# Attention with hash buckets and a small expert layer: whole-array shapes for two products, float16 experts, pairs of chunks on GpSimd

## The chip, the cores and the metric

The kernel runs on one core of a Trainium2 chip. The core has five engines with instruction streams of their own: TensorE (PE), VectorE (DVE), ScalarE (ACT), GpSimd (POOL) and SyncE (SP). They meet at semaphores. SBUF is the on-chip memory of 128 partitions, PSUM the memory that PE writes its products to, and queues carry DMA between device memory and SBUF. The metric is the device time of one execution in microseconds (us); lower is better.

## The reference

Inputs are q, k and v of shape (4, 8, 768, 64), that is 4 batches of 8 heads, 768 tokens and 64 dimensions, all float32, a projection of 64 by 6, a gate vector of 512, and the expert's weights w1 (512 by 1024) and w2 (1024 by 512).

```python
q_bucket = sum over 6 bits of (q @ proj > 0) * 2**bit       # k_bucket likewise
mask = q_bucket[..., :, None] == k_bucket[..., None, :]
scores = where(mask, q @ k.T / 8, -1e9)
scores = scores - max(scores, -1)
attn = exp(scores);  attn = attn / (sum(attn, -1) + 1e-9)
x = attn @ v                                # regrouped as (4, 768, 512)
for b in range(4):
    s = x[b] @ w_gate
    top = the 128 tokens of the highest s
    ye = relu(x[b, top] @ w1) @ w2
    out[b, top] = x[b, top] + sigmoid(s[top]) * ye     # other tokens: out = x
```

So there are 32 heads of attention with a mask, and after every eighth head one choice of 128 tokens and one small expert layer on them. Since the chosen tokens depend on a ranking of float32 sums, the kernel carries its products in pieces: a high part and a low part of float16 or bfloat16 stand for one float32.

## The kernel before, in words

**One head.** `load_x` brings q and k of a head, transposed, as one 128 by 768 tile X. `hash_half` and `signs` form the hash bits as +-8192 rows. `split_xh` (ACT) and `split_xl` (DVE, line 235) cut X into float16 parts XH and XL, and SP's DMAs place these in the operands A and B of a head (`place_a`, `place_b`). A score product over A thus holds the dimensions and the hash bits at once, so that equal buckets stand far above all others.

*The maxima.* For each of six chunks t of 128 queries `max_unit` makes two products mx of 384 columns; `max_relu` (ACT, line 348) takes the relu of the one, a difference of two halves of keys, and `max_red` (DVE, line 356, the rows mj) adds the other and leaves the maximum in a column of m. `max_turn` (line 365) turns m (128 by 6) with one product mt into six rows, `max_copy` (ACT) copies them into mr, and `max_row` sends them with a DMA of SP into row 96 of A. The difference of halves that A needs is `k_diff` (DVE, line 334, xd).

*The scores.* `st_unit` makes transposed scores st (keys in partitions) in nine units of 512 columns, each one product over A (line 385) and one over B (389); the row of maxima must be in A before the head's first. `st_exp` (ACT, lines 403 and 405) writes the exponentials into P, a float32 tile of two chunks of 128 keys, three units to a pair of chunks.

*The sum over v.* P is used as its upper 16 bits (read in place as bfloat16) and a rest R, P minus those 16 bits, as float16. `r_chunk` (line 418) makes R for each of the six chunks of keys, on DVE or on POOL; the table `POOL_R` names the chunks that POOL takes, by even and odd head. `av` multiplies both with v's parts (line 442, three products of 65 or 64 columns for each chunk and tile of queries) on top of a seed (line 428): a product of `zs` and `W` that starts all 396 columns of the accumulator with a multiple of the sum of v. `W` is 33 rows: row 0 holds the high part of that sum, row 32 the low part (`sum_hi`, `sum_lo`, line 319). `recip` (DVE, 452 to 454, the rows rc) and `norm` (ACT, line 467) divide.

**One batch.** `score` (DVE, line 484, rows jks) forms the gate's sums as heads finish. `choose` ranks 768 tokens by comparing every score with every other (lines 528 to 536, rows cm and eq), turns the rank into an index and gathers the 128 tokens with POOL's indirect DMA (606). `expert` does the layer: `turn_x` transposes the tokens (xp); `split_x` makes a float32r high part, a float32r rest and a bfloat16 copy; `up` (662) multiplies the tokens' parts with w1's parts, with the tokens as the stationary operand and 512 columns of w1 moving: 12 products for each half of the 1024 hidden values; `relu`, then `turn_h` transposes the hidden values with four products per half (674), `split_h` and `split_h2` cut them, `down` (700) multiplies with w2's parts, and `finish` (707) scales, adds and scatters. The experts of batches 0 and 1 are stepped between the heads of later batches, that of batch 2 runs at the end, and that of batch 3 must wait for the last head (`rank_last`, `apply_expert_last`).

**What sets the order.** Every step above is put on one list by a due time: head h starts its scores at 9h, and each kind of step has an offset in a table T. The steps are issued in the order of these due times, and every engine runs its own instructions in exactly that order. `mine` marks a DVE instruction, and `turn` makes the next POOL instruction wait for the one marked last. `LEAD` is how far the maxima run ahead of the scores, `AVLAG` how far `av` runs behind.

## Time and profile before

| | |
| - | - |
| time, median of 3 runs | 487.26 us (485.84 to 487.91) |
| the profiled execution | 488.31 us, of which the span of instructions is 486.5 |
| mean granted PE clock | 0.956 |
| busy: PE, DVE, ACT, POOL | 430.6, 396.5, 344.0, 171.7 us |
| largest groups on DVE | R 119.5, mj 106.2 us |
| largest groups on ACT | exponentials 113.2 and 58.0, relu 95.3 us |

A row of a group names the line, the engine, the operation, out<-in by the program's names, the shape, the count, the busy time and the mean of one in ns, and the idle time ahead of it with what ended it. A row of the timeline names the start in us, the duration, and in brackets the wait ahead of the instruction. Matmul rows include the pipeline's tail, so their starts, not their durations, tell how fast PE takes them. L418 is line 418 of the kernel.

### The profile page before, as it was taken

The page shows a single profiled execution, that of the slowest core. Times are in us where ns is not written, and L with a number is a line of the kernel's source. Part 1 is how long each engine was busy: PE and PEld are TensorE (multiplying, and loading weights), DVE is VectorE, ACT ScalarE, POOL GpSimd, SP SyncE. Part 2 cuts the span into 40 slices and gives each one's busy share as a digit, 9 for nine tenths or more (in the row PEclk, how much of TensorE's full clock was granted, in tenths as well). Part 3 has the DMA queues.
Part 4 walks back from the last instruction along what each step waited for, and adds up shares of the span by engine and source line. Part 5 has one row for each costly group of instructions (what it writes and reads, how often), then busy time and mean ns, then how long its engine had stood idle before and what let it go on. Part 6 is the DMA issues. An engine that isn't in the chain of part 4 may idle for free. (4 is left out here: it accounts for less than half of the span.)

```text
span 486.5 us, 14126 instructions
## 1 busy us (share of the span) xinstructions
PE 430.6 (89%) x5379; PEld 283.9 (58%) x5393; DVE 396.5 (81%) x991; ACT 344.0 (71%) x826; POOL 171.7 (35%) x137
## 2 busy tenths in 40 slices
PE   4789999978997898999998889899897899998795
PEld 3146666555654665676656566566565666666463
DVE  5669989999999997777799999999999977656611
ACT  2588898889885876787777579698775778763312
POOL 7025654445463352222413242324242333232300
PEclk9689999999999798999999899999998889999999
DMA  4774535545663233342464226445531133102010
GB/s 127 235 200 131 168 100 169 179 123 136 197 190 96 81 112 98 120 111 67 143 186 123 77 66 169 140 127 137 157 111 44 30 106 98 34 2 88 2 43 22
DMA packets 36167, 55.30 MB, mean 114 GB/s; under 512 B 6194, under 2 KB 27396, under 8 KB 36100
## 3 DMA queue, kind: packets, MB, share of 16 engines
q1 hardware_dynamic: 24676, 34.85, 26.2%
...
## 5 line engine op out<-in xcount | busy, mean ns | idle before, releaser
L418 POOL TENSOR_TENSOR R<-P 128x768 f16<-128x768 f32 x80 | 124.9, 1562 | 246.9 <-DVE xd L334 95.1
L403 ACT ACTIVATE P<-st 128x512 f32<-128x512 f32 x192 | 113.2, 608 | 37.1 <-PE st L389 35.2
L442 PEld LDWEIGHTS <-P 128*128 128x128 bf16 x2304 | 120.1, 99 | 30.2 <-issue 20.3
L442 PE MATMUL av<-V,P 128*128 128x65 f16 (+1 forms) x2304 | 128.0, 196 | 0.0
L442 PE MATMUL av<-V,R 128*128 128x65 f16 x1152 | 123.1, 194 | 3.9 <-POOL R L418 2.3
L418 DVE TENSOR_TENSOR R<-P 128x768 f16<-128x768 f32 x112 | 119.5, 1067 | 7.0 <-ACT P L405 6.8
L385 PE MATMUL st<-A 97*128 97x256 f16 (+1 forms) x384 | 123.4, 333 | 0.3
L389 PE MATMUL st<-B 128*128 128x256 f16 (+1 forms) x384 | 123.3, 333 | 0.0
L356 DVE CUSTOM_DVE_ANT_0 mj<-mx,me 128x384 bf16<-128x384 f32 x192 | 106.2, 553 | 20.8 <-PE mx L340 8.4
L348 ACT ACTIVATE me<-mx 128x384 f32<-128x384 f32 x192 | 95.3, 497 | 28.7 <-DVE m L356 14.0
L442 PEld LDWEIGHTS <-R 128*128 128x128 f16 x1152 | 108.5, 100 | 5.2 <-POOL R L418 2.7
L340 PE MATMUL mx<-K,A 96*128 96x384 f16 x192 | 60.7, 344 | 10.4 <-DVE oneb L159 4.7
L405 ACT ACTIVATE P<-st 128x512 f32<-128x512 f32 x96 | 58.0, 604 | 11.3 <-PE st L389 10.0
L340 PE MATMUL mx<-A 96*128 96x384 f16 x192 | 64.6, 338 | 1.4 <-ACT me L348 0.7
L340 PEld LDWEIGHTS <-A 96*128 96x128 f16 x384 | 36.3, 100 | 30.0 <-issue 12.2
L467 ACT ACTIVATE x<-av,rc 128x64 f32<-128x64 f32 x192 | 42.2, 311 | 12.1 <-DVE rc L454 11.9
L385 PEld LDWEIGHTS <-A 97*128 97x128 f16 x384 | 38.1, 99 | 21.2 <-issue 7.2
L389 PEld LDWEIGHTS <-B 128*128 128x128 f16 x384 | 38.3, 100 | 18.7 <-issue 1.9
L235 DVE SCALAR_TENSOR_TENSOR XL<-X,XH 128x768 f16<-128x768 f32 x32 | 39.7, 1242 | 2.3 <-DMA B<-XL 2.3
L230 ACT ACTIVATE XH<-X 128x768 f16<-128x768 f32 x32 | 27.1, 850 | 7.6 <-DMA X<-in_qk_dram 7.6
L203 PE MATMUL hp<-X,pjt 128*32 128x384 f32 x128 | 17.6, 524 | 1.9 <-DMA X<-in_qk_dram 1.8
L334 DVE TENSOR_TENSOR xd<-XH 64x384 f16<-64x384 f16 x32 | 12.7, 397 | 8.0 <-ACT XH L230 7.1
...
## 6 DMA issues: line engine op xcount, KB each, us to landing
...
```

Source lines behind the costliest of these rows:

```text
L230: nc.scalar.activation(xh, st["X", h], AF.Copy, scale=XS)
L235: mine(nc.vector.scalar_tensor_tensor(xl, st["X", h], XS, st["XH", h], op0=ALU.mult, op1=ALU.subtract))
L340: nc.tensor.matmul(pt[:, :384], a[0:96, 0, t * P : (t + 1) * P], a[0:96, 1, 384:768] if i else K[h % NA][0:96], start=True, stop=True,)
L348: nc.scalar.activation(me, st["mx", h, t, 0][:, :384], AF.Relu)
L356: nc.vector.tensor_tensor_reduce(out=jk, in0=st["mx", h, t, 1][:, :384], in1=st["me", h, t], op0=ALU.add, op1=ALU.max, scale=1.0 / MS, sca ...
L385: nc.tensor.matmul(pt[:, o : o + n], a[:, 1, c * P : (c + 1) * P], a[:, 0, q0 : q0 + n], start=True, stop=False,)
L389: nc.tensor.matmul(pt[:, o : o + n], bt[:, 1, c * P : (c + 1) * P], bt[:, 0, q0 : q0 + n], start=False, stop=True,)
L403: nc.scalar.activation(pp[:, r, 0:512], pt, AF.Exp, scale=ES)
L405: nc.scalar.activation(pp[:, :, 512:768], pt.rearrange("p (a b) -> p a b", a=2), AF.Exp, scale=ES)
L418: (turn if pool else mine)(eng.tensor_tensor(t, pp[:, r, :], hi_view(pp, r), op=ALU.subtract))
L442: nc.tensor.matmul(o[:, t, 0:n], l, vv[:, c, hh, v0 : v0 + n], start=False, stop=last and l is lo, skip_group_check=True,)
L467: nc.scalar.activation(x[:, t], o[:, t, 0:D], AF.Copy, scale=rc[:, t : t + 1])
```

## The change

**Shapes.** m is now one of two fixed 128 by 128 tiles M, zero but for six columns, so that the turning product has all 128 rows of output; the seed reads 65 rows of zs and W instead of 33, with the low part in row 64 (both are cleared at the start).

**Experts.** w1 and w2 are kept as a float16 part and a bfloat16 rest. The tokens are scaled by 16 and cut into two float16 parts. `up` now has the weights as the stationary operand and the tokens moving, 128 columns each: 48 products for each half, and the hidden values come out transposed, so `turn_h` is gone. `split_h` takes relu and high part on ACT and the rest on DVE. `down` has its 24 products of 512 columns as before.

**R.** POOL takes R in pairs of chunks with one instruction of 128 by 1536: chunks 2 and 3 of an even head, chunks 0, 1 and 4, 5 of an odd one. DVE takes the others, one chunk per instruction. R's tiles hold a pair, four of them.

**Order.** All of T is new, with LEAD, AVLAG and AVS, and the junk tile of mj has two buffers.

Three places in the order of the instructions show what moved. The first is DVE in head 22 and the start of head 23's work; R22_2 is the rest of head 22's chunk 2, mj24_1 the second chunk of maxima of head 24. Before:

```order
L418 TENSOR_TENSOR R22_0_6520<-P22_0_6442 128x768
L356 ISA mj23_5_6524,m23_6294<-mx23_5_1_6515,me23_5_6513 128x384
L334 TENSOR_TENSOR xd26_6530<-XH26_6522 64x384
L452 TENSOR_SCALAR rc21_6568<-av21_6344 128x6
L356 ISA mj24_0_6574,m24_6573<-mx24_0_1_6564,me24_0_6562 128x384
L235 SCALAR_TENSOR_TENSOR XL25_6580<-X25_5542,XH25_6240 128x768
L418 TENSOR_TENSOR R22_2_6604<-P22_1_6528 128x768
L356 ISA mj24_1_6606,m24_6573<-mx24_1_1_6599,me24_1_6597 128x384
L418 TENSOR_TENSOR R22_3_6644<-P22_1_6528 128x768
```

And now:

```order
L241 SCALAR_TENSOR_TENSOR XL25_6524<-X25_5251,XH25_6163 128x768
L462 TENSOR_SCALAR rc21_6528<-av21_6330 128x6
L362 ISA mj24_1_6534,M0_79<-mx24_1_1_6526,me24_1_6520 128x384
L362 ISA mj24_2_6539,M0_79<-mx24_2_1_6532,me24_2_6522 128x384
L362 ISA mj24_3_6575,M0_79<-mx24_3_1_6566,me24_3_6563 128x384
L426 TENSOR_TENSOR R22_2_6613<-P22_2_6536 128x768
L362 ISA mj24_4_6663,M0_79<-mx24_4_1_6632,me24_4_6628 128x384
L362 ISA mj24_5_6665,M0_79<-mx24_5_1_6634,me24_5_6630 128x384
L362 ISA mj25_0_6682,M1_80<-mx25_0_1_6678,me25_0_6676 128x384
L340 TENSOR_TENSOR xd27_6689<-XH27_6680 64x384
```

XL has moved ahead of three rc and three mj, and one R stands where three stood; the R of chunks 2 and 3 has left DVE. (Rows that read an accumulator, the other rc and score rows are left out; the last number of a name in the R rows of the change counts pairs.)

The second place is POOL at the same heads. Before:

```order
L418 TENSOR_TENSOR R22_1_6566<-P22_0_6442 128x768
L418 TENSOR_TENSOR R22_4_6697<-P22_2_6608 128x768
L418 TENSOR_TENSOR R23_1_6816<-P23_0_6708 128x768
L418 TENSOR_TENSOR R23_2_6854<-P23_1_6778 128x768
L418 TENSOR_TENSOR R23_4_6948<-P23_2_6858 128x768
```

And now:

```order
L429 TENSOR_TENSOR R22_1_6561<-P22_1_6435 128x1536
L429 TENSOR_TENSOR R23_0_6674<-P23_0_6606 128x1536
L429 TENSOR_TENSOR R23_2_6879<-P23_2_6784 128x1536
L429 TENSOR_TENSOR R24_1_7079<-P24_1_6947 128x1536
```

Five instructions of one chunk have become three of two. Each waits for the DVE instruction marked last ahead of it: the first for XL25 above, the second for the R ahead of mj24_4.

The third place is DVE at the end: sc3 are the last batch's scores, ye2 the result of batch 2's expert, cm3 the ranking of batch 3. Before:

```order
L842 TENSOR_TENSOR sc3_2_9190<-sc3_2_9190,sc3_1_9000 128x6
L653 TENSOR_SCALAR ss2_9181<-ss2_9181 128x1
L692 TENSOR_TENSOR htl2_9244<-ht2_0_9238,hth2_9243 128x512
L528 TENSOR_SCALAR cm3_0_9257,cnt3_9256<-sbc3_9205,sc3_2_9190 128x640
L882 TENSOR_SCALAR idx3_9331<-ip3_9318 128x1
L692 TENSOR_TENSOR htl2_9244<-ht2_1_9297,hth2_9243 128x512
L707 SCALAR_TENSOR_TENSOR ye2_9354<-yp2_9268,ss2_9181,xe2_8097 128x512
```

And now:

```order
L805 TENSOR_TENSOR sc3_2_9168<-sc3_2_9168,sc3_1_8948 128x6
L684 SCALAR_TENSOR_TENSOR htl2_9174<-mh2_0_9116,hth2_9173 128x512
L684 SCALAR_TENSOR_TENSOR htl2_9174<-mh2_1_9177,hth2_9173 128x512
L661 TENSOR_SCALAR ss2_9112<-ss2_9112 128x1
L701 SCALAR_TENSOR_TENSOR ye2_9279<-yp2_9230,ss2_9112,xe2_8139 128x512
L538 TENSOR_SCALAR cm3_0_9284,cnt3_9283<-sbc3_9244,sc3_2_9168 128x640
```

The whole expert of batch 2 now stands ahead of the ranking of batch 3, which it followed and was mixed with.

The diff, cut to its core:

```diff
+EX = 16.0
+KZ = 65
-LEAD = 14
-AVLAG = 3
+LEAD = 14.39
+AVLAG = 4.79
-AVS = ((0, 9, 1.1), (9, 18, 2.34), (18, 27, 5.75), (27, 36, 6.91))
+RB = 4
+AVS = ((0, 9, 1.9), (9, 18, 3.66), (18, 27, 5.56), (27, 36, 6.99))
 T = dict(
-    loadx=-34.22, hash=-5.11, hash2=4.23, sign=0.81, xh=-11.6, xl=-1.02, pa=-4.18, ps=2.13, loadv=-16.35,
+    loadx=-40.48, hash=-4.07, hash2=1.42, sign=1.08, xh=-10.75, xl=1, pa=-0.1, ps=2.23,
...
-POOL_R = ((1, 4), (1, 2, 4))
+POOL_R = ((1,), (0, 2))
...
-    zs = cp.tile([33, P], BF16, name="zs")
+    zs = cp.tile([KZ, P], BF16, name="zs")
+    M = [cp.tile([P, P], F16, name=f"M{i}") for i in range(2)]
...
-    w1h = cp.tile([P, 4, FF], F32R, name="w1h")
+    w1h = cp.tile([P, 4, FF], F16, name="w1h")
...
-        w = W[pr % 2][32:33, :, 0 : D + 1]
+        w = W[pr % 2][64:KZ, :, 0 : D + 1]
...
-            st["m", h] = sb.tile([P, NC], F16, tag="m", name=f"m{h}", bufs=2)
-        jk = sb.tile([P, 384], BF16, tag="jks", name=f"mj{h}_{t}", bufs=1)
+            st["m", h] = M[h % 2]
+        jk = sb.tile([P, 384], BF16, tag="jks", name=f"mj{h}_{t}", bufs=2)
...
-        nc.tensor.matmul(pt[:NC, :P], st["m", h], ident16, start=True, stop=True)
+        nc.tensor.matmul(pt[:, :P], st["m", h], ident16, start=True, stop=True)
...
     def r_chunk(h, c):
-        need(("e", h, 3 * (c // 2) + 2))
-        pp, r = st["P", h, c // 2], c % 2
-        t = sb.tile([P, S], F16, tag="R", name=f"R{h}_{c}", bufs=6)
-        pool = c in POOL_R[h % 2]
-        eng = nc.gpsimd if pool else nc.vector
-        (turn if pool else mine)(eng.tensor_tensor(t, pp[:, r, :], hi_view(pp, r), op=ALU.subtract))
-        st["R", h, c] = t
+        g, r = divmod(c, 2)
+        need(("e", h, 3 * g + 2))
+        pp = st["P", h, g]
+        if r == 0:
+            st["R", h, g] = sb.tile([P, 2, S], F16, tag="R", name=f"R{h}_{g}", bufs=RB)
+        t = st["R", h, g]
+        if g not in POOL_R[h % 2]:
+            mine(nc.vector.tensor_tensor(t[:, r], pp[:, r], hi_view(pp, r), op=ALU.subtract))
+        elif r == 0:
+            a = slice(0, 2)
+            turn(nc.gpsimd.tensor_tensor(t, pp, hi_view(pp, a), op=ALU.subtract))
...
-                st["O", h], zs, W[h // 2 % 2][:, hh].unsqueeze(1).broadcast_to([33, NC, OW]),
+                st["O", h], zs, W[h // 2 % 2][:, hh].unsqueeze(1).broadcast_to([KZ, NC, OW]),
...
         def split_x():
             xp = t["xp"]
-            xh, xl, xb = tile_("xth", 512, F32R), tile_("xtl", 512, F32R), tile_("xtb", 512, BF16)
-            nc.scalar.copy(xh, xp)
-            nc.vector.tensor_tensor(xl, xp, xh.bitcast(F32), op=ALU.subtract)
-            nc.scalar.copy(xb, xh.bitcast(F32))
-            t["x"] = ((xh, w1h), (xl, w1h), (xb, w1l))
-            t["hs"] = tile_("hs", FF, F32)
+            xh, xl = tile_("xth", 512, F16), tile_("xtl", 512, F16)
+            nc.scalar.activation(xh, xp, AF.Copy, scale=EX)
+            nc.vector.scalar_tensor_tensor(xl, xp, EX, xh, op0=ALU.mult, op1=ALU.subtract)
+            t["x"] = ((xh, w1h), (xl, w1h), (xh, w1l))
...
+        def up(hp, e, fs, order=(0, 1, 2)):
+            for i in order:
+                x, w = t["x"][i]
+                for f in fs:
+                    o = e * 512 + f * P
+                    for k in range(4):
+                        nc.tensor.matmul(
+                            hp[:, f * P : (f + 1) * P], w[:, k, o : o + P],
+                            x[:, k * P : (k + 1) * P],
+                            start=(f == 0 and k == 0 and i == order[0]),
+                            stop=(k == 3 and i == order[-1]), skip_group_check=True,
+                        )
+        def split_h(hp, e):
...
+            nc.scalar.activation(hh[:, f], hp, AF.Relu)
+            nc.vector.scalar_tensor_tensor(
+                hl[:, f], hp, 0.0, hh[:, f], op0=ALU.max, op1=ALU.subtract
+            )
...
     def apply_expert_last(b, tags, bank, bank2):
...
-        m.up(h0, 0, range(4), (0, 2, 1), True)
-        m.relu(h0, 0)
-        m.up(h1, 1, range(2), (0, 2, 1), True)
-        m.turn_h(bank(f"ht{b}_0"), 0)
...
+        m.up(h0, 0, range(4), (0, 2, 1))
+        m.split_h(h0, 0)
+        m.up(h1, 1, range(4), (0, 2, 1))
+        m.split_h(h1, 1)
```

More of the change, by code (lines that the diff above doesn't have):

```diff
@@ L103, in body @@
     ones16 = cp.tile([P, P], F16, name="ones16")
-    zs = cp.tile([33, P], BF16, name="zs")
-    W = [cp.tile([33, 2, OW], F16, name=f"W{i}") for i in range(2)]
+    zs = cp.tile([KZ, P], BF16, name="zs")
+    W = [cp.tile([KZ, 2, OW], F16, name=f"W{i}") for i in range(2)]
+    M = [cp.tile([P, P], F16, name=f"M{i}") for i in range(2)]
     iota16 = cp.tile([P, P], F16, name="iota16")
@@ L126, in init_first @@
             nc.gpsimd.memset(crow[:, i], c)
+        for t in M:
+            nc.gpsimd.memset(t, 0.0)
     def init_a(i):
@@ L482, in score @@
             st["scd", b, part, t] = True
-            jk = sb.tile([P, 384], BF16, tag="jks", name=f"jks{b}_{part}_{t}", bufs=1)
+            jk = sb.tile([P, 384], BF16, tag="jks", name=f"jks{b}_{part}_{t}", bufs=2)
             i = nc.vector.tensor_tensor_reduce(
@@ L652, in gate2 @@
             ss = t["ss"]
-            nc.vector.tensor_scalar(ss[:, 1:2], ss[:, 1:2], 1.0, None, op0=ALU.add)
+            nc.vector.tensor_scalar(ss[:, 1:2], ss[:, 1:2], 1.0, EX, op0=ALU.add, op1=ALU.mult)
             nc.vector.reciprocal(ss[:, 1:2], ss[:, 1:2])
-        def up(hp, e, ks, order=(0, 1, 2), by_part=False):
-            ki = [(k, i) for k in ks for i in order]
-            if by_part:
-                ki = [(k, i) for i in order for k in ks]
-            for k, i in ki:
-                l, r = t["x"][i]
-                nc.tensor.matmul(
-                    hp, l[:, k * P : (k + 1) * P], r[:, k, e * 512 : e * 512 + 512],
-                    start=(k == 0 and i == order[0]), stop=(k == 3 and i == order[-1]),
-                )
@@ L667, in relu @@
-        def relu(hp, e):
-            nc.scalar.activation(t["hs"][:, e * 512 : e * 512 + 512], hp, AF.Relu)
-        def turn_h(tp, e):
-            t["tp", e] = tp
-            for k in range(4):
-                o = e * 512 + k * P
-                nc.tensor.transpose(
-                    out=tp[:, k * P : (k + 1) * P], in_=t["hs"][:, o : o + P], identity=ident
-                )
-        def split_h(e):
-            if e == 0:
-                t["h"] = [
-                    (tile_("hth", FF, F32R), w2h), (tile_("htl", FF, F32R), w2h),
-                    (tile_("htb", FF, BF16), w2l),
-                ]
-            (hh, _), (hl, _), (hb, _) = t["h"]
-            f, tp = slice(e * 512, e * 512 + 512), t["tp", e]
-            nc.scalar.copy(hh[:, f], tp)
-            nc.scalar.copy(hb[:, f], hh[:, f].bitcast(F32))
@@ L711, in finish @@
             )
-        for f in (turn_x, split_x, gate, gate2, up, relu, turn_h, split_h, split_h2, down, finish):
+        for f in (turn_x, split_x, gate, gate2, up, split_h, down, finish):
             setattr(m, f.__name__, f)
@@ L717, in body @@
     MAIN = dict(
-        xth=("M3", 1), xtl=("M2x", 1), xtb=("M2", 2), hs=("M0", 1), hth=("M1", 1),
-        htl=("M2x", 1), htb=("M3", 1), ye=("jk", 1),
+        xth=("M3", 1), xtl=("M2x", 1), hth=("M1", 1), htl=("M0", 1), ye=("jk", 1),
     )
-    LATE = dict(MAIN, htl=("X", XB), htb=("V", 1), ye=("X", XB))
+    LATE = dict(MAIN, ye=("X", XB))
     LAST = dict(
-        xth=("XH", XHB), xtl=("XL", XLB), xtb=("R", 6), hs=("P", 4), hth=("P", 4),
-        htl=("P", 4), htb=("P", 4), ye=("X", XB),
+        xth=("XH", XHB), xtl=("XL", XLB), hth=("P", 4), htl=("P", 4), ye=("X", XB),
     )
@@ L747, in apply_expert @@
             hp = mo_bank(f"mh{b}_{e}")
-            for k in range(4):
-                m.up(hp, e, (k,))
+            for f in range(4):
+                m.up(hp, e, (f,))
                 yield 1
-            m.relu(hp, e)
-            yield 2
-        for e in range(2):
-            m.turn_h(mo_bank(f"ht{b}_{e}"), e)
-            yield 1
-            m.split_h(e)
-            yield 0.5
-            m.split_h2(e)
-            yield 1.5
+            m.split_h(hp, e)
+            yield 0.5 + e
         yp = mo_bank(f"yp{b}")
@@ L857, in rank_last @@
             for i in range(3 * e, 3 * e + 3):
-                eq = sb.tile([P, P], F32, tag="R", name=f"eq{b}_{i}", bufs=6)
+                eq = sb.tile([P, P], F32, tag="eql", name=f"eq{b}_{i}", bufs=6)
                 eqs.append(eq)
```

72 lines of the change are left out of this document (25 added, 47 removed).

## Prediction, made before the changed kernel ran

> **What bounds the kernel now.** I read the windows first: busy time of each engine by stretch, in the order PE, PEld, DVE, ACT, POOL, then granted clock.
>
> ```profile
> 40.00:180.00 140.00, 123.93 (x1747) 83.17 (x1745) 132.26 (x305) 114.38 (x280) 67.92 (x44) 0.98 0.49 139
> 200.00:240.00 40.00, 39.59 (x488) 26.66 (x489) 30.81 (x72) 30.73 (x76) 12.76 (x9) 1.00 0.33 92
> 240.00:380.00 140.00, 125.62 (x1788) 84.85 (x1787) 132.17 (x340) 108.36 (x268) 43.12 (x28) 0.98 0.44 123
> 400.00:440.00 40.00, 39.66 (x496) 27.02 (x498) 25.79 (x72) 28.28 (x68) 12.73 (x8) 1.00 0.14 42
> ```
>
> In 40 to 180 and 240 to 380 DVE is busy 132 of 140 us, 94%, while ACT has 114 and 108 and PE's 124 and 126 count each matmul's pipeline tail. These 280 us are DVE's. Where the experts of batches 0 and 1 run (200 to 240, 400 to 440) PE has 39.6 of 40 and DVE 31 and 26: those are PE's. After 440 nothing is full; a chain of dependent steps (rank, gather, last expert) sets the end. Then I asked what DVE's time consists of, by shape (busy, mean ns) and by tile (min/median/max ns).
>
> ```profile
> L418 DVE TENSOR_TENSOR R<-P 128x768 f16<-128x768 f32 x112 | 119.5, 1067 | 7.0 <-ACT P L405 6.8
> L235 DVE SCALAR_TENSOR_TENSOR XL<-X,XH 128x768 f16<-128x768 f32 x32 | 39.7, 1242 | 2.3 <-DMA B<-XL 2.3
> L286 DVE SCALAR_TENSOR_TENSOR V<-V,V 128x768 f16<-128x768 f32 x16 | 19.0, 1186 | 0.0
> ...
> L418 DVE TENSOR_TENSOR R<-P x112: 946/955/2241, 29.5 to 443.0; 128x768 f16<-128x768 f32 x112
> ...
> L225 DVE TENSOR_TENSOR sd<-sg x10: 345/1034/1605, 7.9 to 356.1; 128x384 f16<-128x384 f16 x7, 32x384 f16<-32x384 f16 x2, 64x384 f16<-64x384 f16 x1
> ```
>
> The means lie far over the minima, and the timeline (start, duration, then in brackets the wait before it) shows why:
>
> ```profile
> 303.66 0.96 DVE L418 TENSOR_TENSOR R<-P 128x768 f16<-128x768 f32 x1
> 304.53 0.42 DVE L484 CUSTOM_DVE_ANT_0 jks<-x,wgt 128x256 bf16<-128x256 f32 x1
> ...
> 306.23 1.47 POOL L418 TENSOR_TENSOR R<-P 128x768 f16<-128x768 f32 x1 [4.81 <-DVE xd L334]
> 307.12 1.39 DVE L235 SCALAR_TENSOR_TENSOR XL<-X,XH 128x768 f16<-128x768 f32 x1
> ...
> 315.25 0.56 DVE L356 CUSTOM_DVE_ANT_0 mj<-mx,me 128x384 bf16<-128x384 f32 x1 [0.17 <-DVE m L356]
> ```
>
> POOL's R ends at 307.70; the XL that DVE began at 307.12 ends at 308.51, 0.81 later. R, of the same 768 columns, has been as short as 0.946; XL took 1.39, because it stood still until POOL was done. A DVE instruction with two SBUF inputs loses what is left of POOL's. The price of this now: R 112 x (1067 - 946) = 13.6, XL 32 x (1242 - 946) = 9.5, V 16 x (1186 - 946) = 3.8, sd 10 x (1034 - 345) = 6.9, together 34 us.
>
> **The change, part by part.** *R.* DVE gives 16 of its 112 R to POOL. An R costs its 0.87 us step (303.66 to 304.53). How many of them lie where DVE sets the pace, the windows of this line on DVE alone tell:
>
> ```profile
> 40.00:180.00 140.00, 44.20 (x39) 0.98 0.49 139
> 240.00:380.00 140.00, 40.14 (x40) 0.98 0.44 123
> ```
>
> 79 of 112, a share of 0.7, which I take for everything that comes per head. So 11.3 R count: -9.8 us. The other 4.7 are worth nothing, DVE has time there.
>
> *The lock.* POOL now has 48 instructions of 1536 elements instead of 80 of 768. No row shows one. Bounds: 1.47 us, if it cost nothing more, and 2.94, twice that; I take 2.8, near the doubled row. What counts is DVE's work without a second SBUF input behind the instruction that releases POOL. From the order: in an even head XL now stands ahead, then three rc and three mj. Today's place had POOL at 306.23 and XL at 307.12, a cover of 0.89 with one mj; two more at 0.73 (0.56 and the 0.17 ahead of it, at 315.25) make 2.35, a stall of 0.45. In an odd head the first pair has three mj and then xd, the second mj, W, mj, mj: about 2.1 each, 0.7 stalled. With one pair in an even and two in an odd head that is 0.62 on average; a score op among them, in somewhat over a quarter, takes off its 0.43: 0.51. In the stretches are 34 of the 48: 17.3 us. Today's are 34 x 0.7 = 23.8. So about -6, with bounds at -24 (no stall at all) and +41 (the rival below).
>
> Since POOL's pair ends later, products that use R come later too (AVLAG 3 to 4.79); between POOL's release and the product lie 3 to 6 us of PE work in the order, more than 2.8, so that costs 0. The second junk buffer frees the 0.17 wait between two mj, but the order has 77 such neighbours instead of 43; I take 0, from -2 to +6 (34 more at 0.17).
>
> *Whole-array shapes.* PE's start times:
>
> ```profile
> 203.65 0.38 PE L389 MATMUL st<-B 128*128 128x512 f16 x1
> 203.96 0.34 PE L428 MATMUL av<-W,zs 33*128 33x396 f16 x1
> 204.23 0.24 PE L442 MATMUL av<-V,P 128*128 128x65 f16 x2
> ...
> 205.06 0.48 PE L662 MATMUL mh<-w1h,xth 128*128 128x512 f32 x1
> ...
> 205.62 0.39 PE L662 MATMUL mh<-w1l,xtb 128*128 128x512 bf16 x1
> 205.85 0.33 PE L340 MATMUL mx<-K,A 96*128 96x384 f16 x1
> ...
> 210.20 0.22 PE L297 MATMUL sp<-V,ones 128*128 128x130 f16 x1
> 210.26 0.22 PE L301 MATMUL sp<-V,ones 128*128 128x128 f16 x1
> ...
> 214.97 0.33 PE L340 MATMUL mx<-A 96*128 96x384 f16 x1
> 215.22 0.22 PE L365 MATMUL mt<-ident,m 128*6 128x128 f16 x1
> 215.37 0.28 PE L385 MATMUL st<-A 97*128 97x256 f16 x1
> ```
>
> A 512-column step is about 0.23 (205.62 to 205.85). Around the seed it is 0.31 and 0.27 (396 columns are worth 0.18), around the turning product 0.25 and 0.15 (384 and 128 columns: 0.17 and 0.06). Each form of less than the whole array thus costs some 0.18 beyond its columns, 0.37 a head. At 6 heads in PE's 80 us that is -2.2; in DVE's stretches it is hidden (DVE is full there), and if DVE's cover went, it would be worth up to 9 more.
>
> *Experts.* Now a k costs 0.79 (205.06 to 205.85), 16 of them make 12.6 us. Two turns of h, four float32 transposes each as in xp (467.96 below: 0.60, of which 0.16 is a matmul's end, 0.22 - 0.06 at 210.20), cost 0.44 each: 13.5 in all. After: the first layer has 96 matmuls of 128 columns with a fresh weight each; the nearest rows, sums over V with a weight load for every product, step 0.06: 5.6 us. The second layer keeps 24 of 512, at 0.22: 5.3. So 2.6 less per expert, twice in PE's stretches: -5.2. ACT loses the copies to float and bfloat (off the path: ACT is busy 31 of 40 us there). DVE's subtractions stay. If the float32 weight loads were already hidden the gain falls to 1.
>
> The Trainium skill speaks against this (TensorE: Matmul & The Clock Gate, "Back-to-back issue gap"): in a stream of weight loads and matmuls it gives about 81 ns at 128 columns. By that the first layer would take 7.8 instead of 5.6, in four experts, two of them in the tail: the sum would come to about 474 (an estimate by that page); the 0.06 of this trace decides.
>
> *Tail.*
>
> ```profile
> 444.71 0.17 DVE L452 TENSOR_SCALAR rc<-av 128x6 f32<-128x6 f32 x1 [0.76 <-PE av L442]
> 453.06 0.87 DVE L528 TENSOR_SCALAR_CACHE_REDUCE cm<-sbc,sc 128x640 bf16<-128x640 f32 x1
> 460.42 0.16 DVE L882 TENSOR_SCALAR idx<-ip 128x1 int32<-128x1 f32 x1 [0.27 <-PE ip L878]
> ...
> 467.96 0.60 PE L628 MATMUL xp<-cs,xe 128*128 128x128 f32 x4
> 481.39 0.75 DVE L707 SCALAR_TENSOR_TENSOR ye<-yp,ss,xe 128x512 f32<-128x512 f32 x1 [2.80 <-PE yp L700]
> ...
> DMA to landing us min/median/max: 3.4/3.4/3.4
> ```
>
> The order now puts all of expert 2, with ye2 on DVE, ahead of the last ranking. Today comparing starts 8.3 after the last av's division (444.71 to 453.06). Now PE first has 5.6, the twelve float32 transposes that spread the scores (at xp's 0.11: 1.3) and 5.3; then a matmul's end of 0.4 and ye2's 0.75: 13.4, so +5.1. The gather, issued once the index is there and landing 3.4 later, was hidden behind expert 2 and is bare now: xp at 460.42 + 5.1 + 0.16 + 3.4 = 469.1, 1.1 later. The last expert took 13.4 from xp to ye; 0.6 + 5.6 + 5.3 and an estimated 0.8 for the copies between make 12.3. Sum 0, from -2 to +4 (PE waits 7 us in the ranking, and a lower clock may follow).
>
> **Sum.** Against this execution's 488.31 (span 486.5 and 1.8 around it; the median of the runs shown is 487.26): -9.8 - 6 - 2.2 - 5.2 + 0 = -23.2, so **465**. The start (loads and hashing, ahead of 40 us) keeps its steps.
>
> **Rivals.** *POOL's longer hold decides.* If the exponentials release POOL late, after mj have already passed, the cover is again 0.89 and each of the 34 stalls DVE for 1.9: 65 us against 23.8, +41, and with the other terms (-17.2) 512: slower. It decides from (23.8 + 17.2) / 34 = 1.2 us of stall each. For it: the XL at 307.12 is one of 32 whose mean is 0.3 over R's minimum, so today's order does not avoid collisions; against: in a stretch where DVE is last, the exponentials are ready and DVE itself releases POOL, as xd does at 306.23. The Trainium skill (SBUF — State Buffer, "SBUF: two separate sides") calls the pair of ports an exclusive lock held for the whole instruction; the 1.39 agrees, so a doubled POOL instruction is a doubled hold.
>
> *The row of maxima.* From the turning product the row goes through a copy and a DMA to the head's first score. At the start of the kernel nothing else runs there:
>
> ```profile
> 22.90 0.27 PE L365 MATMUL mt<-ident,m 128*6 128x128 f16 x1 [0.24 <-DVE m L356]
> ...
> 25.27 0.58 PE L385 MATMUL st<-A 97*128 97x512 f16 x1
> ```
>
> That is 2.4 us at least. In the order PE's work between the two falls from about 4.7 to 3.1 us. If ACT and SP add 1.4 to the 2.4, PE waits 0.7 in each of 32 heads, 22 us, and most is eaten: 487. *Half.* Collisions stay at today's 23.8 and the experts give 1 instead of 5.2, or the 9.8 of R is lost in waits on PE: 475 both ways. *Better.* POOL fits into its cover nearly everywhere, 7 us of stalls instead of 17: 455.
>
> **Chances.** Forecast 0.53 (own range 459 to 472), half 0.21, better 0.10, the row 0.08, POOL's hold 0.08. The range goes from better to beyond half: 452 to 484, which leaves out the last two and a little of the edges. Faster than 487.26 by over 0.5% (about what a measurement of this kernel tells from none): the first three, 0.84; the row makes 0.08 the same; POOL's hold 0.08 slower.
>
> **What would show it.** Right: DVE's R near 0.95 x 96, POOL's R near 2.8 x 48, xd grown to about 1.1 in odd heads and XL back at 0.95; steps around seed and turn of 0.23 and 0.17; the first layer at 0.06 a matmul; xp some 24 us behind the last division. Wrong: R, xd or XL of over 2 us in numbers; PE waiting ahead of st for the row; DVE idle over 10% in the middle.

## The result, and the profile after

The changed kernel takes 467.81 us, the median of four runs (467.56 to 468.68), against 486.55 for the kernel before on the same chip. The ratio is 0.9628 (0.9584 to 0.9673). The forecast was 465 with a range of 452 to 484. The profiled execution took 468.68 (span 466.9), 19.6 less than the profiled one of before.

First the windows, in the prediction's columns (PE, PEld, DVE, ACT, POOL, granted clock):

```profile
40.00:180.00 140.00, 124.29 (x1838) 87.19 (x1835) 127.21 (x309) 117.51 (x290) 67.95 (x32) 1.00 0.52 150
240.00:380.00 140.00, 126.75 (x1877) 90.55 (x1874) 131.33 (x350) 112.34 (x277) 48.97 (x19) 0.98 0.42 119
```

DVE is still the fullest engine of both stretches (127 and 131 of 140 us, where it had 132 twice), and more heads pass through each of them. The groups of DVE and POOL by shape (count, busy, mean ns):

```profile
L429 POOL TENSOR_TENSOR R<-P 128x1536 f16<-128x1536 f32 x48 | 132.0, 2751 | 212.8 <-DVE R L426 45.2 <-PE st L395 39.9 <-DVE rc L462 35.3
L426 DVE TENSOR_TENSOR R<-P 128x768 f16<-128x768 f32 x96 | 98.1, 1043 | 0.5
L241 DVE SCALAR_TENSOR_TENSOR XL<-X,XH 128x768 f16<-128x768 f32 x32 | 32.5, 1014 | 1.6 <-DMA B<-XL 1.3
L340 DVE TENSOR_TENSOR xd<-XH 64x384 f16<-64x384 f16 x32 | 15.7, 492 | 6.7 <-ACT XH L236 5.8
L292 DVE SCALAR_TENSOR_TENSOR V<-V,V 128x768 f16<-128x768 f32 x16 | 15.5, 970 | 0.0
L494 DVE CUSTOM_DVE_ANT_0 jks<-x,wgt 128x256 bf16<-128x256 f32 x24 | 14.9, 622 | 0.0
L543 DVE SCALAR_TENSOR_TENSOR eq<-sbc,sc,cs 128x128 f32<-128x128 f32 x21 | 13.5, 642 | 0.0
L494 DVE CUSTOM_DVE_ANT_0 jks<-x,wgt,sc 128x256 bf16<-128x256 f32 x18 | 11.7, 698 | 0.0
L601 DVE TENSOR_SCALAR sel<-iota,rank 128x128 f16<-128x128 f16 x18 | 8.4, 521 | 0.1
L231 DVE TENSOR_TENSOR sd<-sg 128x384 f16<-128x384 f16 x7 | 2.8, 406 | 0.2
```

A pair on POOL takes 2.75 us, near the 2.8 that was assumed. XL, V and sd have lost nearly all of their stalls, as the order says they should. But in the kernel before, the same view had these rows for the other instructions that could collide:

```profile
L334 DVE TENSOR_TENSOR xd<-XH 64x384 f16<-64x384 f16 x32 | 12.7, 397 | 8.0 <-ACT XH L230 7.1
L484 DVE CUSTOM_DVE_ANT_0 jks<-x,wgt 128x256 bf16<-128x256 f32 x24 | 10.0, 416 | 0.0
L484 DVE CUSTOM_DVE_ANT_0 jks<-x,wgt,sc 128x256 bf16<-128x256 f32 x18 | 8.7, 483 | 1.2
L533 DVE SCALAR_TENSOR_TENSOR eq<-sbc,sc,cs 128x128 f32<-128x128 f32 x21 | 8.0, 381 | 0.0
L591 DVE TENSOR_SCALAR sel<-iota,rank 128x128 f16<-128x128 f16 x18 | 7.1, 461 | 0.1
```

jks went from 416 and 483 ns to 622 and 698, eq from 381 to 642, xd from 397 to 492. One such case from the timeline of the changed kernel:

```profile
267.56 2.75 POOL L429 TENSOR_TENSOR R<-P 128x1536 f16<-128x1536 f32 x1 [4.10 <-DVE R L426]
268.66 1.79 DVE L543 SCALAR_TENSOR_TENSOR eq<-sbc,sc,cs 128x128 f32<-128x128 f32 x1
```

POOL's pair ends at 270.31, the eq that began at 268.66 ends at 270.45 and has taken 1.79 us for some 0.35 of work. The stalls have moved to other instructions. To sum them over all of DVE's instructions, take what each lasts beyond the median of its shape, where that is over 0.1 us (the medians are those of four runs together: before, the change, the short hold and both old, as named below). The sum is 38.7 us before and 35.3 in the change, and every instruction counted runs beside one of POOL.

PE's steps around the seed, around the turning product and in the experts' first layer:

```profile
200.42 0.33 PE L438 MATMUL av<-W,zs 65*128 65x396 f16 x1
200.59 0.23 PE L452 MATMUL av<-V,P 128*128 128x65 f16 x2
...
203.08 0.39 PE L670 MATMUL mh<-xtl,w1h 128*128 128x128 f16 x4
203.30 0.39 PE L670 MATMUL mh<-xth,w1l 128*128 128x128 f16 x4
...
208.95 0.22 PE L371 MATMUL mt<-ident,M 128*128 128x128 f16 x1
209.00 0.33 PE L346 MATMUL mx<-K,A 96*128 96x384 f16 x1
```

The seed steps 0.17 (0.27 before), the turning product 0.055 (0.15), and four products of the first layer with their weight loads take 0.22, 0.056 each.

The start and the end:

```profile
26.13 0.73 SPq L248 DMA_DIRECT2D A<-mr  x1
28.24 0.59 PE L391 MATMUL st<-A 97*128 97x512 f16 x1 [3.20 <-DMA A<-mr]
...
423.74 0.17 DVE L462 TENSOR_SCALAR rc<-av 128x6 f32<-128x6 f32 x1 [0.22 <-PE av L452]
436.28 0.87 DVE L538 TENSOR_SCALAR_CACHE_REDUCE cm<-sbc,sc 128x640 bf16<-128x640 f32 x1
443.64 0.16 DVE L845 TENSOR_SCALAR idx<-ip 128x1 int32<-128x1 f32 x1 [0.28 <-PE ip L841]
447.54 1.09 PE L638 MATMUL xp<-cs,xe 128*128 128x128 f32 x4 [0.51 <-DMA xe<-out_dram,idx]
461.72 0.75 DVE L701 SCALAR_TENSOR_TENSOR ye<-yp,ss,xe 128x512 f32<-128x512 f32 x1 [3.60 <-PE yp L694]
```

The first head's scores wait for its row of maxima until 28.24 (25.27 before): SP issues it behind a load of X and three DMAs of head 2. At the end comparing starts 12.5 us after the last division (8.3 before), xp follows the index by 3.9 (7.5 before), and the last expert takes 14.2 from xp to ye (13.4 before), its xp 1.09 instead of 0.60.

To see where the time went, the span is cut at the first exponential of head 0 and at that of head 31 (of nine exponentials per head, on ACT), for each kernel in its profiled execution; the last column is the sum of DVE's stalls, counted as above:

| kernel | head 0 begins | head 31 begins | between | from there to the end | DVE's stalls |
| - | - | - | - | - | - |
| before | 26.3 | 428.4 | 402.1 | 58.1 | 38.7 |
| the change | 29.3 | 408.4 | 379.1 | 58.5 | 35.3 |
| before, experts alone | 26.7 | 426.2 | 399.5 | 51.6 | 38.4 |
| before, shapes alone | 26.6 | 424.7 | 398.1 | 57.9 | 39.6 |
| change, old order and old share | 26.5 | 424.6 | 398.1 | 51.6 | 40.1 |
| change, old order | 26.2 | 445.1 | 418.9 | 51.5 | 53.0 |
| change, old share | 28.6 | 433.4 | 404.8 | 56.6 | 55.2 |
| change, pairs as two singles | 28.9 | 410.7 | 381.8 | 56.4 | 35.1 |
| change, one junk buffer | 29.6 | 413.8 | 384.2 | 56.5 | 30.9 |
| change, short hold | 28.6 | 388.5 | 359.9 | 58.2 | 5.1 |
| change with two repairs | 28.2 | 408.3 | 380.1 | 52.9 | 36.8 |

The heads give 23.0, the start takes 3.0 and the end 0.4. The lower rows are the experiments. Each row is one execution: that of before lies 1.8 us above the median of its runs, that of both old 3.4 above, that of the old order 3.7 below.

### The profile page after: what moved, and what is told of

Its sections match the earlier page's. It is cut to its first block, busy times and chain, and to the rows that moved or that the text cites. A ratio compares the mean times of both kernels' runs of the same rounds, so it can differ in the third digit from the quotient of the medians.

```text
span 466.9 us, 14615 instructions
## 1 busy us (share of the span) xinstructions
PE 412.9 (88%) x5649; PEld 287.6 (62%) x5649; DVE 372.4 (80%) x975; ACT 330.3 (71%) x806; POOL 177.6 (38%) x107
## 3 DMA queue, kind: packets, MB, share of 16 engines
q1 hardware_dynamic: 24676, 34.85, 26.2%
q10 hardware_dynamic: 10592, 17.44, 12.1%
## 5 line engine op out<-in xcount | busy, mean ns | idle before, releaser
L429 POOL TENSOR_TENSOR R<-P 128x1536 f16<-128x1536 f32 x48 | 132.0, 2751 | 212.8 <-DVE R L426 45.2
L362 DVE CUSTOM_DVE_ANT_0 mj<-mx,me 128x384 bf16<-128x384 f32 x192 | 102.8, 553 | 29.2 <-PE mx L346 17.2
L452 PE MATMUL av<-V,P 128*128 128x65 f16 (+1 forms) x2304 | 124.8, 195 | 0.0
L452 PE MATMUL av<-V,R 128*128 128x65 f16 x1152 | 120.5, 193 | 0.0
L354 ACT ACTIVATE me<-mx 128x384 f32<-128x384 f32 x192 | 90.3, 496 | 42.8 <-PE mx L346 21.9
L426 DVE TENSOR_TENSOR R<-P 128x768 f16<-128x768 f32 x96 | 98.1, 1043 | 0.5
L346 PE MATMUL mx<-A 96*128 96x384 f16 x192 | 55.7, 337 | 8.9 <-DVE M L362 5.2
L241 DVE SCALAR_TENSOR_TENSOR XL<-X,XH 128x768 f16<-128x768 f32 x32 | 32.5, 1014 | 1.6 <-DMA B<-XL 1.3
L340 DVE TENSOR_TENSOR xd<-XH 64x384 f16<-64x384 f16 x32 | 15.7, 492 | 6.7 <-ACT XH L236 5.8
L438 PE MATMUL av<-W,zs 65*128 65x396 f16 x32 | 10.8, 336 | 10.0 <-ACT x L477 10.0
```

The costliest lines, as they stand in the source:

```text
L241: mine(nc.vector.scalar_tensor_tensor(xl, st["X", h], XS, st["XH", h], op0=ALU.mult, op1=ALU.subtract))
L346: nc.tensor.matmul(pt[:, :384], a[0:96, 0, t * P : (t + 1) * P], a[0:96, 1, 384:768] if i else K[h % NA][0:96], start=True, stop=True,)
L354: nc.scalar.activation(me, st["mx", h, t, 0][:, :384], AF.Relu)
L362: nc.vector.tensor_tensor_reduce(out=jk, in0=st["mx", h, t, 1][:, :384], in1=st["me", h, t], op0=ALU.add, op1=ALU.max, scale=1.0 / MS, sca ...
L426: mine(nc.vector.tensor_tensor(t[:, r], pp[:, r], hi_view(pp, r), op=ALU.subtract))
L429: turn(nc.gpsimd.tensor_tensor(t, pp, hi_view(pp, a), op=ALU.subtract))
```

## The experiments

**The share of R and the order, each undone alone and both together.** The old order in the changed kernel:

```diff
-LEAD = 14.39
+LEAD = 14
-AVLAG = 4.79
+AVLAG = 3
 T = dict(
...
+    (all of T, and AVS, as before)
```

> All of the changed code, with the old order (T, LEAD, AVLAG and AVS of before). POOL's pairs then start behind the DVE instructions that released single chunks before. If the rival 'POOL's longer hold decides' is right and the new order is what avoids it, each of the 34 pairs in DVE's stretches stalls DVE for some 1.9 us and the time is about 467.8 + 65 - 17 = 515. If the stalls move from one kind of DVE instruction to another whatever the order is (the changed kernel's trace: R, XL, V and sd stall less, jks, eq, xd and sel more, the sum about as before), the time stays within 10 us of 467.8; the start then gets back some 3 us (the row of the first head is issued 2.6 us earlier in the old order) and the tail some 3.

Measured: 502.29 (498.62 to 506.23; without the longest of the four runs the median is 500.44), ratio 1.0376 (1.0317 to 1.0434). The heads take 39.8 more than with the new order. The row of the products with R in the change, then two rows of this kernel:

```profile
L452 PE MATMUL av<-V,R 128*128 128x65 f16 x1152 | 120.5, 193 | 0.0
...
L452 PE MATMUL av<-V,R 128*128 128x65 f16 x1152 | 123.6, 194 | 15.5 <-POOL R L429 15.3
L340 DVE TENSOR_TENSOR xd<-XH 64x384 f16<-64x384 f16 x32 | 29.7, 929 | 8.8 <-ACT XH L236 8.0
```

xd stands still for long in 14 of the 32 heads (6 in the change; its mean is 929 ns instead of 492), and PE waits 15.3 us for POOL's R (nothing in the changed kernel). The time comes nearly three quarters of the way to the 515 of the rival in which POOL's hold decides, and not near the 10 of the other theory. But only a part of it goes that rival's way: of the 39.8 in the heads DVE's stalls make 17.7 at the most (53.0 against 35.3, counted over the whole kernel), and PE's wait for R was no part of the rival. To a kernel with pairs the new order is worth some 34 us. The run undoes all of the order at once, so it does not tell the place of the pairs from LEAD and AVLAG.

The old share in the new order:

```diff
-        if g not in POOL_R[h % 2]:
+        if c not in POOL_R[h % 2]:
             mine(nc.vector.tensor_tensor(t[:, r], pp[:, r], hi_view(pp, r), op=ALU.subtract))
-        elif r == 0:
+        else:
-            turn(nc.gpsimd.tensor_tensor(t, pp, hi_view(pp, a), op=ALU.subtract))
+            turn(nc.gpsimd.tensor_tensor(t[:, r], pp[:, r], hi_view(pp, r), op=ALU.subtract))
-POOL_R = ((1,), (0, 2))
+POOL_R = ((1, 4), (1, 2, 4))
```

> The changed kernel with the old share of R: POOL takes chunks 1 and 4 of even heads and 1, 2 and 4 of odd heads, one chunk per instruction, and DVE has 112 instead of 96. By the prediction's term 11.3 R x 0.87 come back, and by the rows of the changed kernel (14 of the 16 lie in DVE's stretches) 12: 478 to 480, if the stalls stay. If the pairs cost as much by their stalls as they take off DVE, it stays at 468.

Measured: 493.60 (492.13 to 496.15), ratio 1.0187 (1.0152 to 1.0222): 26 us slower than the change, outside both expectations and twice what 16 R cost. The other half is in the row of R:

```profile
L426 DVE TENSOR_TENSOR R<-P 128x768 f16<-128x768 f32 x112 | 132.6, 1194 | 0.4 <-ACT P L411 0.4
```

1194 ns, 151 more than in the changed kernel, which is 17 us over 112. 32 of them take over 1.1 us (14 in the change), and 30 of these 32 run beside an R of POOL: its single chunks now start where DVE's R come next.

Both undone together (the two diffs above in one):

> The changed kernel with the old order and also the old share of R (POOL takes chunks 1 and 4 of even heads, 1, 2 and 4 of odd heads, one by one): what is left of the change are the shapes, the experts and the second junk buffer. If order and share are one change that only pays as a whole (new order with old share 493.6, old order with pairs 502.3, both new 467.8), this kernel is near the kernel before, less what experts and shapes give: 478 to 484. If the new order is good for itself and the old share bad for itself, it is slower than both, over 502.

Measured: 474.55 (473.24 to 477.98), ratio 0.9735 (0.9663 to 0.9807). So, against the change, the new order with the old share costs 26, the old order with the new share 34, and both old ones together only 7 (5 by the ratios), which is below the 478 to 484 that were expected of this kernel. They are one change: the price of each depends on the other. In the heads the two are worth 19 by the table (some 16, with each execution set back to the median of its runs), but the new order gives 7 back at the end and 3 at the start.

**Pairs as two single instructions.**

```diff
         elif r == 0:
-            turn(nc.gpsimd.tensor_tensor(t, pp, hi_view(pp, a), op=ALU.subtract))
+            for r in range(2):
+                turn(nc.gpsimd.tensor_tensor(t[:, r], pp[:, r], hi_view(pp, r), op=ALU.subtract))
```

> The changed kernel, but each pair that POOL takes is made with two instructions of 768 elements, one behind the other, both released by the same DVE instruction. DVE's share is unchanged. If the length of POOL's hold sets the stalls, DVE can slip in between the two halves and the stalls of some 32 us in the heads fall by a third or more: 457 to 462. If a DVE instruction that has to wait simply waits for whatever POOL does until both are done, or meets the second half instead, nothing changes: 466 to 470. POOL itself needs 96 x 1.47 = 141 us instead of 132, which is off the path.

Measured: 467.46 (466.45 to 468.85), ratio 0.9624 (0.9598 to 0.9650), no difference from the change. The stalls sum to 35.1 us instead of 35.3: jks and eq lose less (the first jks and eq take 467 and 483 ns instead of 622 and 642), R and XL more. That POOL takes both chunks in one instruction is worth nothing. By the runs above, what counts is which chunks it takes and when.

**What the lock costs.** POOL's instructions cut to a sixth:

```diff
-            turn(nc.gpsimd.tensor_tensor(t, pp, hi_view(pp, a), op=ALU.subtract))
+            turn(nc.gpsimd.tensor_tensor(
+                t[:, :, 0:P], pp[:, :, 0:P], hi_view(pp, a)[:, :, 0:P], op=ALU.subtract
+            ))
...
+            tl = 0 if c // 2 in POOL_R[h % 2] else t
-            lo = st["R", h, c // 2][:, c % 2, t * P : (t + 1) * P]
+            lo = st["R", h, c // 2][:, c % 2, tl * P : (tl + 1) * P]
```

> The changed kernel, but each of POOL's 48 instructions for R makes 128 of the 768 columns of each chunk of its pair, and the products that use POOL's chunks read these 128 columns for all six tiles of queries: five sixths of POOL's R are left out, and the sums are not the attention's. All instructions, waits and products are as many as before; only POOL's hold falls from 2.75 us to about 0.5. In the two stretches that DVE sets, its instructions stood still for 18.0 and 13.6 us behind POOL. If these 31.6 us are what the lock costs, the time falls to some 438 to 445. If PE (busy 36 of 40 us there) takes over after a part, 450 to 456. If the stalls are waits that something else would fill, 464 to 468.

Measured: 447.81 (446.93 to 448.94), ratio 0.9220 (0.9195 to 0.9245). Its rows:

```profile
40.00:180.00 140.00, 130.79 (x1918) 91.64 (x1912) 119.82 (x326) 124.22 (x308) 31.91 (x35) 0.99 0.56 160
```

```profile
L426 DVE TENSOR_TENSOR R<-P 128x768 f16<-128x768 f32 x96 | 90.5, 964 | 0.8 <-ACT P L411 0.4
L340 DVE TENSOR_TENSOR xd<-XH 64x384 f16<-64x384 f16 x32 | 12.0, 374 | 6.4 <-ACT XH L236 5.5
L497 DVE CUSTOM_DVE_ANT_0 jks<-x,wgt 128x256 bf16<-128x256 f32 x24 | 10.0, 418 | 0.0
L497 DVE CUSTOM_DVE_ANT_0 jks<-x,wgt,sc 128x256 bf16<-128x256 f32 x18 | 7.8, 482 | 0.0
L546 DVE SCALAR_TENSOR_TENSOR eq<-sbc,sc,cs 128x128 f32<-128x128 f32 x21 | 7.3, 347 | 0.0
L604 DVE TENSOR_SCALAR sel<-iota,rank 128x128 f16<-128x128 f16 x18 | 3.8, 268 | 0.1
```

With a short hold, R, jks, eq, xd and sel are near their own lengths, and the stalls sum to 5.1 us instead of 35.3. That is 20.0 us of time for some 31 us of stalls (against the rows of the change: 96 x 79 ns of R, 24 x 204 and 18 x 216 of jks, 21 x 295 of eq, 18 x 253 of sel, 32 x 118 of xd), between the first and the second expectation; then PE is the fullest engine (130.8 of 140). A short hold also makes POOL's R ready earlier, but that is not the gain: in the change the products with R already wait for nothing (0.0 in their row, shown at the old order). So the lock is real and still costs 20 us in the changed kernel.

**Score instructions marked** (on the kernel of the two repairs below): `MINE_SC = True`.

> The kernel of the two repairs (463.4) with the score instructions marked too, so that a POOL pair that stood ahead of a score instruction starts behind it. jks stands still for 9.8 us in the changed kernel. If that can be avoided for itself, 457 to 460. If the stall only moves to the next instruction with two SBUF inputs, 462 to 465.

Measured: 475.39 (473.87 to 477.75), ratio 0.9784 (0.9751 to 0.9817): 12 slower than without, outside both expectations. jks stalls less (24 and 18 of them, together about 3 us less) and R more (its mean goes to 1102 ns, +6 us over 96), as the second expectation had it, but DVE also stands idle ahead of mj for 9 us more:

```profile
L362 DVE CUSTOM_DVE_ANT_0 mj<-mx,me 128x384 bf16<-128x384 f32 x192 | 102.7, 553 | 29.5 <-PE mx L346 17.6 <-ACT me L354 9.3 <-ACT XH L236 1.4
L362 DVE CUSTOM_DVE_ANT_0 mj<-mx,me 128x384 bf16<-128x384 f32 x192 | 102.8, 552 | 38.2 <-PE mx L346 21.5 <-ACT me L354 13.5 <-ACT XH L236 1.4
```

The first row is the kernel of the two repairs, the second this one. DVE waits for PE's mx and ACT's me; why they come later was not followed further.

**The parts that were costed for themselves.** Experts alone, in the kernel before (`split_x`, `up`, `split_h`, the weights' types and the three ways to run an expert as in the change):

```diff
-    w1h = cp.tile([P, 4, FF], F32R, name="w1h")
+    w1h = cp.tile([P, 4, FF], F16, name="w1h")
...
-        for e in range(2):
-            m.turn_h(mo_bank(f"ht{b}_{e}"), e)
```

> The kernel before with the float16 experts alone (weights stationary, no turn of h). By the prediction's term 2.6 us per expert, of which the two in PE's stretches count: 480 to 482 (-5.2). In the changed kernel the heads of the first expert's stretch gained only 1.5 and those of the second's 1.2 to 3.2: by that -3 to -4.7. If a product of 128 columns with a fresh weight took 81 ns, 0.4 per expert: 486.

Measured: 479.79 (479.21 to 480.97), ratio 0.9864 (0.9790 to 0.9938), about -6.6. The profiled executions are 8.8 apart, and by the table only 2.6 of that lie in the heads. The end is 6.5 shorter: xp follows the index by 3.9 instead of 7.5, since it no longer waits for expert 2 there, and the last expert takes 12.1 instead of 13.4.

Shapes alone, in the kernel before (M, KZ = 65 and the whole turning product):

```diff
+KZ = 65
...
-        nc.tensor.matmul(pt[:NC, :P], st["m", h], ident16, start=True, stop=True)
+        nc.tensor.matmul(pt[:, :P], st["m", h], ident16, start=True, stop=True)
```

> The kernel before with the shapes alone: the turning product from a 128 by 128 tile, the seed over 65 rows. The steps around both fall by 0.37 us a head (0.31 and 0.26 around the seed, 0.26 and 0.15 around the turn, to 0.22, 0.17, 0.11 and 0.06). If only the six heads in PE's stretches count: -2.2 (484). If PE's steps count in all heads: -12 (475). If they are hidden everywhere: 0.

Measured: 484.29 (481.38 to 487.11, ten runs), ratio 0.9959 (0.9914 to 1.0004): -2.0, not quite to be told from nothing, and clearly not the 12 of all heads.

One junk buffer in the change:

```diff
-        jk = sb.tile([P, 384], BF16, tag="jks", name=f"mj{h}_{t}", bufs=2)
+        jk = sb.tile([P, 384], BF16, tag="jks", name=f"mj{h}_{t}", bufs=1)
```

> The changed kernel with one junk buffer for mj and jks instead of two. By the prediction's term the second buffer is worth 0 (-2 to +6 stood for its range). If the 0.17 us between neighbouring mj count in DVE's stretches, 77 x 0.17 x 0.7 = 9: 477. If the wait is hidden by what mj waits for anyway: 468 to 470.

Measured: 472.35 (471.89 to 473.34), ratio 0.9737 (0.9710 to 0.9765): in the new order the second buffer is worth 4.5, between the two expectations. The row of mj in the change, then in this kernel:

```profile
L362 DVE CUSTOM_DVE_ANT_0 mj<-mx,me 128x384 bf16<-128x384 f32 x192 | 102.8, 553 | 29.2 <-PE mx L346 17.2 <-ACT me L354 9.3 <-ACT XH L236 1.4
L362 DVE CUSTOM_DVE_ANT_0 mj<-mx,me 128x384 bf16<-128x384 f32 x192 | 106.4, 554 | 35.8 <-PE mx L346 14.4 <-ACT me L354 7.0 <-DVE M L362 6.6
```

6.6 us of DVE's idle time ahead of mj end with the reading of the last mj; in the change no such releaser stands there. mj is also busy for 3.6 us more, since with two buffers neighbours overlap. Of these 10 us not quite half reach the time; the stalls behind POOL are 4.4 us fewer with one buffer (30.9).

**The end.** Products without a reader keep PE busy through the last ranking:

```diff
+        wq = st_bank(f"wq{b}")
+        for i in range(14):
+            nc.tensor.matmul(wq, w1h[:, 0, 0:P], w1h[:, 0, 0:512], start=True, stop=True)
...
             count(i, cm, rp)
+            for _ in range((4, 3, 2, 2, 4, 4)[i]):
+                nc.tensor.matmul(wq, w1h[:, 0, 0:P], w1h[:, 0, 0:512], start=True, stop=True)
-WARM = 8
+WARM = 14
```

> The changed kernel, with products on PE that nobody reads, in the wait for the first comparison, behind each count of the last ranking and 14 instead of 8 behind the index. In the changed kernel the last expert's first 32 products step at 0.11 us and the next at 0.056, with a granted clock of 0.75 in the tail. If the slow steps come from PE's idle time in the ranking, they step at 0.056 from the first one, which is 32 x 0.054 = 1.7 us, xp takes 0.6 instead of 1.09, and the time is 465.5. If the clock is low for another reason, 467.8.

Measured: 467.13 (466.84 to 468.54), ratio 0.9622 (0.9601 to 0.9643). Three windows of the change (the ranking up to 443 us, then the index and the 8 products behind it), then one of this kernel (the clock is the sixth value behind the length):

```profile
436.00:439.18 3.18, 0.30 (x6) 0.21 (x7) 3.11 (x10) 0.00 (x0) 1.40 (x2) 1.00 0.20 82
439.18:443.00 3.82, 1.59 (x18) 1.07 (x18) 3.60 (x19) 0.00 (x0) 0.00 (x0) 0.50 0.00 0
443.00:448.00 5.00, 4.49 (x15) 1.80 (x16) 0.52 (x4) 0.00 (x0) 1.00 (x1) 0.50 0.21 52
```

```profile
443.00:448.00 5.00, 5.00 (x30) 2.37 (x29) 1.65 (x11) 0.00 (x0) 1.00 (x1) 1.00 0.11 14
```

From 443 to 448 PE's clock is 1.00 instead of 0.50, xp takes 0.63 instead of 1.09, and the last expert 12.1 from xp to ye instead of 14.2. But the index comes 0.6 later after the last division (counts stand behind the added products), and the median gains 0.7, less than the measurement can tell. The cause of the slow end of the last expert is shown; as a repair it is worth little.

**Two repairs of the order, to see what the start and the end cost.**

```diff
-        at(f + T["turn"] + T["tcopy"] + T["row"], max_row, h)
+        turn0, row0 = (T["turn"], T["row"]) if h else (0.1, 0.02)
+        at(f + turn0 + T["tcopy"] + row0, max_row, h)
...
-    f1=2.13, l0=16.86, l1=10.84, l2=-16.61, l3=14,
+    f1=2.13, l0=6, l1=8.5, l2=1.9, l3=14,
-WARM = 8
+WARM = 12
```

> The changed kernel with two repairs of its order. First, head 0's turning product, row copy and row DMA are put right behind its last maximum, and the load of X for head 6 behind them, so that SP issues the row at some 23.7 us and not at 26.13: heads begin 2.5 us earlier. Second, the last ranking starts while expert 2's second layer still runs (l0 6, l1 8.5, l2 1.9; 12 products behind the index): comparing starts some 5.8 us earlier, and PE has work in the ranking, so that the last expert keeps its clock (another 1.5 to 2). If both hold, 458 to 460. If the row's place is hidden by something else, 460 to 462; if PE delays the counts of the ranking by as much as it starts earlier, 463 to 466.

Measured: 463.43 (462.99 to 464.27), ratio 0.9528 (0.9458 to 0.9597). It beats both the kernel before and the change.

```profile
23.44 0.73 SPq L248 DMA_DIRECT2D A<-mr  x1
26.08 0.63 PE L391 MATMUL st<-A 97*128 97x512 f16 x1
...
424.18 0.17 DVE L462 TENSOR_SCALAR rc<-av 128x6 f32<-128x6 f32 x1 [0.81 <-PE av L452]
432.31 0.86 DVE L538 TENSOR_SCALAR_CACHE_REDUCE cm<-sbc,sc 128x640 bf16<-128x640 f32 x1
456.03 0.75 DVE L701 SCALAR_TENSOR_TENSOR ye<-yp,ss,xe 128x512 f32<-128x512 f32 x1 [3.60 <-PE yp L694]
```

Comparing starts 8.1 after the last division instead of 12.5, the index follows it by 15.9 instead of 19.9, the last expert takes 12.1 instead of 14.2, and the end is 5.6 shorter. By its number the time falls into the third expectation, but not for its reason: the counts are hardly delayed (4.0 of the 4.4 are left at the index). The first score comes 2.2 earlier, its exponential 1.1, but head 31 begins at 408.3 as before: the late row of the first head costs nothing at the end that this run shows, and all of the gain is the end's.

The first comparison ahead of expert 2's second htl (the rest of half of its hidden values), each count one comparison later (on top of the two repairs):

```diff
-    f1=2.13, l0=6, l1=8.5, l2=1.9, l3=14,
+    f1=2.13, l0=6, l1=3, l2=1.9, l3=14,
...
             compare(i, sc, sbc, cm, eqs[i], cnt, i in POOL_EQ)
-            count(i, cm, rp)
+            if i:
+                count(i - 1, cms[i - 1], rp)
...
```

> The kernel of the two repairs (463.4) with the first comparison of the last ranking ahead of the second htl of expert 2 on DVE, and each count on PE one comparison later than its own. The first comparison then starts once the spread scores are copied (some 430.3 instead of 432.3): 461.5 to 462.5. If PE, whose second half of expert 2 waits for that htl, becomes the last to finish, 463.4.

Measured: 462.65 (461.69 to 463.06), ratio 0.9529 (0.9502 to 0.9556): the ratio is that of the kernel of the two repairs, so no difference is shown by it. In the profile the first comparison begins at 430.08 instead of 432.31, but the index comes only 1.1 earlier (438.96 for 440.04): the htl now stands among the comparisons.

## Why the prediction was right, point by point

The time lies near the forecast (467.8 for 465) and the gain came where it was forecast, in the heads. The profiled executions are 19.6 apart: 23.0 gained in the heads, 3.0 lost at the start and 0.4 at the end. But the sum is closer than its terms, and that is luck in part. The shapes came as priced; the experts came at their price for each product, but in the heads only half of it; the lock gave some 2 to 3 of its 6; the second junk buffer and the start were set to 0 and were not. What filled the gap in the heads lies in R's new share together with the order, 16 to 19 where 9.8 and 6 were forecast; how much of it is the order's own no run shows.

| term | predicted | measured |
| - | - | - |
| shapes | -2.2 | -2.0 (alone) |
| experts | -5.2, in PE's stretches | -6.6 (alone); in the profile 2.6 in the heads, 6.5 at the end |
| second junk buffer | 0 | -4.5 (in the new order; against the kernel before not measured) |
| R on POOL, and the lock | -9.8 and -6 | together with the order -7; in the heads -16 to -19, at the end +7, at the start +3 |
| end, start | 0, 0 | +0.4, +3.0 in the profile (the latter without a loss that the repair shows) |

**R.** The step by which 11.3 R count at 0.87 each failed in its form: R has no fixed price. To take the same 16 off DVE costs 28 us in the old order (474.6 to 502.3) and gains 26 in the new one (493.6 to 467.8). What was right is that in the heads they are the largest gain once the order fits. Over the whole kernel, with what the order loses at the start and the end, they are worth about as much as the experts.

**The lock.** Of the terms this one failed most clearly. The stall of each pair was worked out for the four instructions that stalled most before (R, XL, V, sd). These lost what was hoped and more: by the prediction's formula they go from 33 us to 9.3 + 2.2 + 0.4 + 0.4 = 12.3. (The prediction has 34: for sd it used the median of ten instructions of three shapes, and by their means sd lost 6.2 and not 6.9.) But jks, eq, sel and xd, counted against their lengths with a short hold, go from 4.9 to 23.3: 24 x 204 + 18 x 216 + 21 x 295 + 18 x 253 + 32 x 118 ns. Over all of DVE's instructions the stalls go from 38.7 to 35.3 us, and in its two stretches from 32.0 to 29.9, where the prediction had 23.8 and 17.3. More heads pass through the stretches now, so that is some 2 to 3 us less for the same work, not 6. The list of victims was incomplete: each instruction that can be locked out has to stand in the sum, also those that collided little before. The one about the score operations was even booked with the wrong sign ("a score op among them, in somewhat over a quarter, takes off its 0.43"): with two SBUF inputs it is itself what stalls. So of the signs that were named, POOL's 2.75 us and XL's return came (30 of 32 are below 1 us), but R's mean is 1.04 and not 0.95, and xd is long in 6 heads and not in every odd one.

**Junk buffer.** The 0.17 between neighbours was seen and counted, and set to 0 against the 77 neighbours in place of 43. The range (-2 to +6) leaves out the 4.5 that the buffer is worth in the new order. Against the kernel before it was not measured: there mj waited 1.9 us for the last one, and its busy time has fallen from 106.2 to 102.8, so some 5 us at the most were to be had.

**Experts and shapes.** 0.056 a product, 0.17 and 0.055 around seed and turn came as read from the nearest rows. The Trainium skill (TensorE: Matmul & The Clock Gate, "Back-to-back issue gap") has 81 ns for a stream of loads and products of 128 columns; four of them take 0.22 us here, so the measurement decides against it. The shapes alone gave -2.0, which the measurement can hardly tell from nothing. The prediction placed the experts' whole gain in PE's stretches and missed that in the old order the end gains most.

**End.** Comparing starts 4.2 later (5.1 were predicted), xp is 0.55 later after the last division (1.1), both for the reasons given. The last expert was to take 12.3 and took 14.2; the lower clock that was named as a risk is the cause (12.1 at full clock). The new order's end was then worse than the old order's with the same experts by 7. Against the kernel before this does not show, since the faster experts alone would have shortened the end by 6.5: the forecast 0 is what is left of the two.

**Rivals.** With the old order the pairs cost about what the rival of POOL's hold said (502 against 512), though less than half of it came as stalls of DVE; the new order avoids it, as forecast. The row of maxima delayed the first head and hardly another: PE's idle time ahead of st that ends with that DMA is 4.1 us in all, 3.2 of them at the first head.
